# Attention feeding a gated feed-forward: the first batch's keys are finished chunk by chunk, and the first images of the main loop are reordered

## The chip, the cores and the metric

The kernel runs on one core of one Trainium2 chip. The metric is the device time of one execution in microseconds, start-up and end included; the span that a profile shows, from the first to the last instruction, is about 2 us shorter. Runs of both kernels that are compared were made on the same chip, in alternation; the experiments were spread over four chips (runs 1 to 4, 5 to 8, 9 to 11, and 12).

## The reference, cut to what matters

```python
def attention(q, kv, w_sr):                    # q: 4 x 12288 x 128, kv: 4 x 384 x 32 x 128
    kv_pool = kv.reshape(B, 96, 4, 8, 4, C).mean(axis=(2, 4))   # 4 x 4 pixels become one
    k = v = kv_pool.reshape(B, -1, C) @ w_sr                    # 768 keys a batch
    a = softmax(q @ k.T / sqrt(C))
    return a @ v

x = attention(...).reshape(49152, 128)
out = (maximum(x @ w_gate, 0) * (x @ w_val)) @ w_out            # d_ff = 1536
```

The kernel cuts the 49152 query rows into 96 tiles of 512, which it calls images. Each needs scores against six chunks of 128 keys, a product with the values, and the feed-forward part: 12 value products, 12 gate products and 48 out products. It works as a pipeline: in the main loop, the scores of image k, the values of image k-1, the value and gate products of image k-3 and the out products of image k-4 are woven together.

## The kernel before

In what follows PE is TensorE, PEld its weight loads, DVE VectorE, ACT ScalarE, POOL GpSimd. Matmul results stand in banks of PSUM, all other tiles in SBUF. A chunk is 128 keys. Before the loop there is a lead, in which the keys of the first batch come in while nothing else can be done. They come in three pairs of chunks; each pair has four lines (`dh` 0 to 3, 512 KB each), and a key is the sum over four lines and four pixels. TensorE transposes ("turns") lines into a PSUM bank in accumulating mode, which adds them up on the way; the turned sum is copied to SBUF, multiplied with `w_sr` and scaled into `kv16`.

```python
    def turn_open(b, pair):
        kv_Ts[b, pair] = bank([128, 2, 128])               # one bank for both chunks of a pair

    def turn_add(b, pair, lines, first=False, final=False, chunks=(0, 1)):
        n = lines.shape[2]
        for h in chunks:
            for i in range(n):                             # four pixels
                nc.tensor.matmul(kv_Ts[b, pair][:, h], lines[:, h, i], ident, is_transpose=True, ...)
        if final and h == 1:                               # one copy for both chunks
            kvT = work.tile([128, 2, 128], FP32, tag="kvT", bufs=2)
            nc.vector.tensor_copy(kvT, kv_Ts[b, pair])
            kv_Ts[b, pair] = kvT

    def project(b, pair):                                  # one product, one scaling for both
        pr = bank([128, 2, 128])
        nc.tensor.matmul(pr, w_sr_f32, kv_Ts.pop((b, pair)), start=True, stop=True)
        nc.vector.tensor_scalar(kv16[:, b, 2 * pair : 2 * pair + 2, 0:C], pr, 1.0 / (r * r), None, op0=ALU.mult)
# [cut]
    # pair 1: lines 0 and 1 are added on VectorE and turned; so are lines 2 and 3, half by half
    turn_open(0, 1)
    turn_add(0, 1, add_lines(1, 0, nc.vector), first=True)
    attend(0, 0)
    for h in range(2):
        s2 = add_lines(1, 2, nc.vector, slice(h, h + 1))
        turn_add(0, 1, s2, final=True, chunks=[h])
    attend(1, 0)
# [cut: loads of the feed-forward weights, queries of group 1 loaded and transposed by DMA, group 2 loaded]
    project(0, 1)
    scores_of(0, 1)
    turn_values(0, 1)
    scores_of(1, 1)
# [cut: pair 2 in the same way, further scores and values]
    for jc in range(NJC - 2):
        values(2, jc, 0)
    left = [(2, jc, 0) for jc in range(NJC - 2, NJC)]      # value steps left over for the first loop image
    left += [(k, jc, half) for k, half in ((3, 0), (2, 1), (3, 1)) for jc in range(NJC)]
# [cut]
    for k in range(LAG, last + 1):                         # the main loop; LAG is 3, the first image
        for step in range(NFB):                            # 12 steps
            kO, kF = k - LAG - 1, k - LAG
            if k == LAG and step >= NFB - 4:
                out_proj(kF, step - NFB + 4)               # 4 of the out products of image 0, early
            if k == LAG + 1 and step % 3 > 0:
                out_proj(kO, 4 + step - 1 - step // 3)     # the other 8
            if 0 <= kO:
                if kO > 0:
                    out_proj(kO, step)
            # [cut]
            if kF < NT:
                value_proj(kF, step)
            if k == LAG:
                own, left = left[:2], left[2:]
                for kV, jc, half in own:
                    values(kV, jc, half)
                    if jc == NJC - 1:
                        keep_sums(kV, half)                # reciprocal, VectorE
                        keep_values(kV, half, nc.scalar)   # normalising multiplies, ScalarE
```

The softmax here doesn't subtract the row's maximum and nothing guards it: scores larger than these inputs give would overflow.

## Time and profile before

| | before |
|---|---|
| time, median of 3 runs (of 6 with those made beside the changed kernel) | 1047.13 us (1046.61) |
| span of the profiled execution | 1044.4 us |
| TensorE busy | 1032.6 us, 99% |
| from the third loop image on | 10.52 us an image, TensorE full |

The granted clock is the share of its full clock at which TensorE ran. A page of the profile gives the busy time of each engine and the chain of work that ended last. The views by stretch, the timelines of one engine and the waits say what happened when. In a timeline, a line holds start, length, engine, source line, operation, output and input tiles with their shapes, the number of instructions in a row, and in brackets how long the engine had stood still and what released it. The reading in one sentence: the loop is TensorE-bound to a few tenths of a per cent, so only the lead and the first two loop images (some 50 us) can give anything. There, no engine is full from the last line of pair 1 to the first value product, and in the second loop image ScalarE is full while TensorE has gaps.

### The profile page before, as it was taken

The page shows a single profiled execution, that of the slowest core. Times are in us where ns is not written, and L with a number is a line of the kernel's source. Part 1 is how long each engine was busy: PE and PEld are TensorE (multiplying, and loading weights), DVE is VectorE, ACT ScalarE, POOL GpSimd, SP SyncE. Part 2 cuts the span into 40 slices and gives each one's busy share as a digit, 9 for nine tenths or more (in the row PEclk, how much of TensorE's full clock was granted, in tenths as well). Part 3 has the DMA queues.
Part 4 walks back from the last instruction along what each step waited for, and adds up shares of the span by engine and source line. Part 5 has one row for each costly group of instructions (what it writes and reads, how often), then busy time and mean ns, then how long its engine had stood idle before and what let it go on. Part 6 is the DMA issues. An engine that isn't in the chain of part 4 may idle for free.

```text
span 1044.4 us, 26093 instructions
## 1 busy us (share of the span) xinstructions
PE 1032.6 (99%) x9948; PEld 686.1 (66%) x9948; DVE 911.3 (87%) x1670; ACT 907.9 (87%) x1741; POOL 107.9 (10%) x127
## 2 busy tenths in 40 slices
PE   7999999999999999999999999999999999999998
PEld 5566666666666666666666666666666666666665
DVE  3798889898888888898888888999888888888898
ACT  3888888888888888888888888888888888888886
POOL 2000044200000005500000003440000000000000
PEclk9999999999999999999999999999999999999999
DMA  8733254432322335543224144562432322212111
GB/s 301 121 82 72 78 181 136 96 73 56 81 57 61 78 115 144 150 84 80 56 63 86 32 87 132 147 151 52 92 63 55 72 67 52 67 32 67 32 47 47
DMA packets 140254, 92.54 MB, mean 89 GB/s; under 512 B 117728, under 2 KB 118624, under 8 KB 140128
## 3 DMA queue, kind: packets, MB, share of 16 engines
q1 hardware_dynamic: 134544, 77.56, 27.7%
q0 software_dynamic: 5440, 13.24, 7.8%
q8 instruction: 78, 1.28, 0.5%
q14 instruction: 48, 0.39, 0.1%
q10 hardware_dynamic: 144, 0.07, 0.0%
HBM read 52.76 MB, written 25.17 MB: 75 GB/s over the span
## 4 chain that ended last, share of the span: by engine, by line
PE 96%; DMA 2%; SPq 1%; DVE 0%; issue 0%; ACT 0%; DVEq 0%
PE bank_ps L274 24%; PE bank_ps L264 23%; PE bank_ps L253 23%; PE bank_ps L215 12%; PE bank_ps L204 11%; DMA parts<-in_kv_dram 2%; SPq L128 1%; SPq L190 1%; PE bank_ps L168 0%; PE bank_ps L156 0%; DMA xT<-x 0%; DMA kvT<-blocks 0%; ACT aT L205 0%; SPq L93 0%; DVE kvT L163 0%
## 5 line engine op out<-in xcount | busy, mean ns | idle before, releaser
L267 DVE SCALAR_TENSOR_TENSOR hT<-bank_ps,val 128x512 f16<-128x512 f32 x1152 | 759.6, 686 | 100.8 <-ACT val L257 75.9
L257 ACT CAST val<-bank_ps 128x512 f16<-128x512 f32 x1152 | 677.9, 591 | 111.5 <-PE bank_ps L253 109.6
L274 PEld LDWEIGHTS <-hT 128*128 128x128 f16 x4608 | 353.1, 98 | 203.7 <-issue 0.9
L274 PE MATMUL bank_ps<-wo,hT 128*128 128x128 f16 x4608 | 443.6, 219 | 0.0
L253 PE MATMUL bank_ps<-xT,wv 128*128 128x512 f16 x1152 | 436.6, 379 | 0.2 <-DMA xT<-x 0.2
L264 PE MATMUL bank_ps<-xT,wg 128*128 128x512 f16 x1152 | 436.6, 379 | 0.0
L205 ACT ACTIVATE aT<-bank_ps 128x512 f16<-128x512 f32 x576 | 346.0, 604 | 17.0 <-PE bank_ps L204 16.6
L215 PE MATMUL bank_ps<-kv,aT 128*128 128x129 f16 x2304 | 223.2, 220 | 0.0
L215 PEld LDWEIGHTS <-aT 128*128 128x128 f16 x2304 | 177.2, 98 | 68.1 <-issue 0.6
L204 PE MATMUL bank_ps<-qT,kv 128*128 128x512 f16 x576 | 216.4, 379 | 1.1 <-DVE kv L169 0.5
L264 PEld LDWEIGHTS <-wg 128*128 128x128 f16 x1152 | 112.7, 98 | 65.7 <-issue 0.5
L253 PEld LDWEIGHTS <-wv 128*128 128x128 f16 x1152 | 112.7, 98 | 0.8 <-DMA xT<-x 0.3
L231 DVE TENSOR_TENSOR x<-bank_ps,rinv 128x256 f16<-128x256 f32 x188 | 79.7, 424 | 6.5
L78 POOL DMA_DIRECT2D q<-in_q_dram x23 | 12.5, 543 | 567.1 <-DMA qT<-q 567.0
L292 DVE TENSOR_SCALAR o_sb<-bank_ps 128x512 f32<-128x512 f32 (+1 forms) x95 | 64.0, 674 | 1.3 <-PE bank_ps L274 1.3
L139 POOL TENSOR_TENSOR s<-parts 128x512 f32<-128x512 f32 x36 | 45.3, 1269 | 165.1 <-DMA parts<-in_kv_dram 156.0
L204 PEld LDWEIGHTS <-kv 128*128 128x128 f16 x576 | 55.8, 98 | 2.4 <-DVE kv L169 1.4
L223 DVE RECIPROCAL rinv<-bank_ps 128x2 f32<-128x2 f32 x192 | 30.6, 160 | 1.6 <-PE bank_ps L215 1.6
L141 POOL TENSOR_TENSOR s<-s 128x512 f32<-128x512 f32 x18 | 22.8, 1267 | 1.4
L143 POOL TENSOR_TENSOR c<-s 128x256 f32<-128x256 f32 x18 | 13.1, 725 | 1.4
L168 PE MATMUL bank_ps<-kvT,w_sr_f 128*128 128x256 f32 x24 | 7.5, 393 | 2.1 <-DMA kvT<-blocks 1.2
L146 POOL TENSOR_TENSOR kv_s<-c 128x128 f32<-128x128 f32 x18 | 8.2, 455 | 1.4
(38 smaller groups left out, 64.0 us busy)
## 6 DMA issues: line engine op xcount, KB each, us to landing
parts<-in_kv_dram SPq DMA_DIRECT2D x48, 512.0 KB, 6.2
out_dram<-o_sb SPq DMA_DIRECT2D x95, 256.0 KB, 2.1
q<-in_q_dram POOLq DMA_DIRECT2D x23, 512.0 KB, 5.3
kvT<-blocks SPq DMA_DIRECT2D x144, 8.0 KB, 1.8
xT<-x SPq DMA_TRANSPOSE x94, 2.5
q<-in_q_dram SPq DMA_DIRECT2D x1, 768.0 KB, 8.3
wv<-in_moe_w_val_dram POOLq DMA_DIRECT2D x2, 192.0 KB, 4.2
wg<-in_moe_w_gate_dram POOLq DMA_DIRECT2D x2, 192.0 KB, 4.7
```

What stands on the lines that cost most here:

```text
L139: eng.tensor_tensor(s2[:, i], parts[:, 2 * i, h], parts[:, 2 * i + 1, h], op=ALU.add)
L204: nc.tensor.matmul(s_ps, kv16[:, k // NST, jc, 0:C], qT_of(k), start=True, stop=True)
L205: nc.scalar.activation(aTs[k][:, jc, :], s_ps, AF.Exp, scale=qk_scale)
L215: nc.tensor.matmul(x_ps[:, i, :], aTs[k][:, jc, s * 128 : (s + 1) * 128], kv16[:, k // NST, jc, C : 2 * C + 1], start=(jc == 0 and i == 0) ...
L223: nc.vector.reciprocal(rinvs[k, half], x_banks[k, half][:, :, C : C + 1])
L231: nc.vector.tensor_tensor(x16s[k][:, 2 * half : 2 * half + 2, :], x_ps[:, :, 0:C], rinv.to_broadcast([128, 2, C]), op=ALU.mult,)
L253: nc.tensor.matmul(va_ps, wv16[:, fb * 128 : (fb + 1) * 128], xTs[k], start=True, stop=True)
L257: nc.scalar.copy(val, va_ps)
L264: nc.tensor.matmul(g_ps, wg16[:, fb * 128 : (fb + 1) * 128], xTs[k], start=True, stop=True)
L267: nc.vector.scalar_tensor_tensor(hTs[k][:, fb, :], g_ps, 0.0, vals.pop((k, fb)), op0=ALU.max, op1=ALU.mult)
L274: nc.tensor.matmul(o_ps, hTs[k][:, fb, s * 128 : (s + 1) * 128], wo16[:, fb, :], start=first, stop=(fb == NFB - 1), skip_group_check=True,)
L292: nc.vector.tensor_scalar(o_sb, o_ps, 1.0 / X_SCALE**2, None, op0=ALU.mult)
```

## The change

The intent is to shorten the way from a landed line to the first score on its keys, and to spread the loop's first two images so that neither ScalarE nor TensorE has idle bits. It has six parts:

1. Every chunk has a bank, a copy, a product and a scaling of its own.
2. In pairs 1 and 2 the last two lines are turned directly from their landed form. VectorE's sums (lines 0 and 1, and then half of the pixels) no longer touch a late line. GpSimd's share of the sums in pair 2 goes to VectorE.
3. The last scores of the lead stand among the first value products.
4. A normalising multiply of the first loop image is issued a step after its reciprocal.
5. The out products of image 0 all stand in the second loop image.
6. The warm-up uses eight matmuls of 512 columns for 34 of 128, and four such matmuls, called fillers below, stand in waits of the first lines.

```diff
-    def turn_open(b, pair):
-        kv_Ts[b, pair] = bank([128, 2, 128])
...
+    def turn_end(chunk, lines):
+        turn_add(chunk, lines)
+        if chunk % 2 == 0:
+            kv_Ts["pair"] = work.tile([128, 2, 128], FP32, tag="kvT", bufs=2, name="kvT")
+        kvT = kv_Ts["pair"][:, chunk % 2]
+        nc.vector.tensor_copy(kvT, kv_Ts[chunk])
+        kv_Ts[chunk] = kvT
+
+    def project_chunk(jc):
+        pr = bank([128, 128])
+        nc.tensor.matmul(pr, w_sr_f32, kv_Ts.pop(jc), start=True, stop=True)
+        nc.vector.tensor_scalar(kv16[:, 0, jc, 0:C], pr, 1.0 / (r * r), None, op0=ALU.mult)
...
+    def first_lines(pair, dh=0):
+        s2 = work.tile([128, 2, r, C], FP32, tag="kv_s2", bufs=3, name="kv_s2")
+        nc.vector.tensor_tensor(s2, line(pair, dh), line(pair, dh + 1), op=ALU.add)
+        s1 = work.tile([128, r, C], FP32, tag="kv_s1", bufs=2, name="kv_s1")
+        s1 = s1.rearrange("p (h i) c -> p h i c", h=2)
+        nc.vector.tensor_tensor(s1, s2[:, :, 0:2], s2[:, :, 2:4], op=ALU.add)
+        return s1
...
+    s1 = first_lines(1)
+    for h in range(2):
+        turn_add(2 + h, line(1, 2, h), first=True)
+    for h in range(2):
+        turn_add(2 + h, s1[:, h])
+    for h in range(2):
+        turn_end(2 + h, line(1, 3, h))
+    for h in range(2):
+        for half in range(2):
+            values(0, h, half)
+        project_chunk(2 + h)
+    scores_of(0, 1)
+    turn_values(0, 1)
+    scores_of(1, 1)
+    gate = const.tile([128, 1], FP32)
+    nc.gpsimd.tensor_copy(gate, line(2, 2)[:, 0, 0, 0:1])     # holds the weights' loads back
...
+    late = [(2, 5), (3, 4), (3, 5)]
+    left = {0: [(1, jc, half) for jc in range(NJC - 2, NJC) for half in range(2)]}
+    for step, k, half in ((1, 2, 0), (4, 3, 0), (7, 2, 1), (10, 3, 1)):
+        left[step] = [(k, jc, half) for jc in range(NJC // 2)]
+        left[step + 1] = [(k, jc, half) for jc in range(NJC // 2, NJC)]
...
-            if k == LAG and step >= NFB - 4:
-                out_proj(kF, step - NFB + 4)
-            if k == LAG + 1 and step % 3 > 0:
-                out_proj(kO, 4 + step - 1 - step // 3)
             if 0 <= kO:
-                if kO > 0:
-                    out_proj(kO, step)
+                out_proj(kO, step)
...
+            if k * NFB + step in ready:
+                kV, hV = ready.pop(k * NFB + step)
+                keep_values(kV, hV, nc.scalar)
             if k == LAG:
+                if late:
+                    scores(*late.pop(0))
...
+                        if kV == 1:
+                            keep_values(kV, hV)
+                        else:
+                            ready[k * NFB + step + 1] = (kV, hV)
```

## The prediction

> **What bounds the kernel now.** I read the page first: shares of the engines, then the chain that ended last.
>
> ```profile
> PE 1032.6 (99%) x9948; PEld 686.1 (66%) x9948; DVE 911.3 (87%) x1670; ACT 907.9 (87%) x1741; POOL 107.9 (10%) x127
> ...
> PE 96%; DMA 2%; SPq 1%; DVE 0%; issue 0%; ACT 0%; DVEq 0%
> ```
>
> TensorE is busy for 99% of the span and carries 96% of the chain. A change that removes none of its matmuls can only win time in which it waits. So I cut the first 61 us into stretches, at points that exist in both kernels: first kv line landed (5.29), last line of pair 1 landed (17.42), first score of pair 2 (27.18), first value product (31.94), start of the second and third image of the main loop (40.89, 50.25).
>
> ```profile
> 0.00:5.29 5.29, 3.33 (x34) 3.16 (x35) 0.06 (x1) 1.49 (x2) 1.35 (x8) 1.00 0.59 188
> 5.29:17.42 12.13, 9.49 (x71) 6.44 (x72) 5.12 (x12) 3.72 (x8) 0.00 (x0) 1.00 1.00 394
> 17.42:27.18 9.76, 8.32 (x67) 5.80 (x64) 4.67 (x9) 4.55 (x9) 6.09 (x8) 1.00 0.87 230
> 27.18:31.94 4.76, 4.39 (x47) 2.86 (x47) 2.01 (x8) 4.08 (x8) 0.00 (x0) 1.00 1.16 184
> 31.94:40.89 8.95, 8.91 (x87) 5.82 (x85) 7.27 (x18) 7.09 (x18) 0.53 (x1) 1.00 1.01 159
> 40.89:50.25 9.36, 9.17 (x67) 4.96 (x66) 8.00 (x13) 9.36 (x21) 0.00 (x0) 1.00 0.43 74
> 50.25:60.77 10.52, 10.52 (x101) 6.85 (x100) 9.51 (x17) 9.77 (x20) 0.53 (x1) 1.00 0.57 109
> ```
>
> The columns are stretch, length, then busy time of PE, PEld, DVE, ACT, POOL, and granted clock, DMA share, GB/s. To 17.42 the DMA runs at its full 394 to 430 GB/s; nothing can be quicker than its lines. From 17.42 to 31.94 no engine is full: this is latency. From 40.89 to 50.25 ACT is full (9.36 of 9.36). From 50.25 on an image costs 10.52 us, all of it PE. So the end is 994 us after the mark at 50.25, and the question is how far that mark, the first value product of the third image, moves. I call it R. The TensorE work ahead of R is the same set in both kernels, but for four line turns more.
>
> Next, in the order of time, the waits between 17 and 28 us:
>
> ```profile
> 17.51 1.29 DVE L362 TENSOR_TENSOR kv_s<-parts 128x512 f32<-128x512 f32 x2 [1.30 <-DMA parts<-in_kv_dram]
> 19.55 0.42 DVE L163 COPY kvT<-bank_ps 128x256 f32<-128x256 f32 x1 [0.75 <-PE bank_ps L156]
> 20.83 0.42 DVE L169 TENSOR_SCALAR kv<-bank_ps 128x256 f16<-128x256 f32 x1
> 21.74 3.24 ACT L205 ACTIVATE aT<-bank_ps 128x512 f16<-128x512 f32 x6 [4.00 <-PE bank_ps L204]
> 23.61 0.69 DVE L362 TENSOR_TENSOR kv_s<-parts 128x512 f32<-128x512 f32 x1 [1.25 <-DMA parts<-in_kv_dram]
> 27.61 4.50 ACT L205 ACTIVATE aT<-bank_ps 128x512 f16<-128x512 f32 x8 [0.89 <-PE bank_ps L204]
> ```
>
> From landing to first score of pair 1: 17.42 to 21.31, or 3.9 us, through an add of each half (0.69), eight turns, a copy of 256 columns, the product and a scaling of 256; ACT stood still for 4.00. For pair 2: 23.49 to 27.18, 3.7 us. Last, the first image of the loop on ACT:
>
> ```profile
> 35.72 0.63 ACT L229 ACTIVATE x<-bank_ps,rinv 128x128 f16<-128x128 f32 x2 [0.58 <-DVE rinv L223]
> ...
> 38.25 0.63 ACT L229 ACTIVATE x<-bank_ps,rinv 128x128 f16<-128x128 f32 x2 [0.46 <-DVE rinv L223]
> ...
> 40.78 0.63 ACT L229 ACTIVATE x<-bank_ps,rinv 128x128 f16<-128x128 f32 x2 [0.46 <-DVE rinv L223]
> ```
>
> A normalising multiply stands in ACT's queue ahead of the casts and waits for a reciprocal that DVE takes after its products: three steps take 2.53 us (35.72 to 38.25), where ACT alone needs 1.95.
>
> **What the Trainium skill says.** "TensorE: Matmul & The Clock Gate", Part 1, gives starts 106.7 or 426.7 ns apart at 128 or 512 columns on the cold clock, 55.6 or 215.7 once warm, after some 3.4 us of work. The trace agrees: 107 ns between the first 25 warm-up matmuls, then 56; scores 216 apart. The f32 turns start 109 apart, measured here. "PSUM — Partial Sum Buffer", section "PSUM bank collisions raise a hardware error", says that two engines may not touch one bank and quadrant at once. That is why before, with both chunks in one bank, the copy waits for the second chunk, and why own banks are needed to overlap; the trace fits (copy at 19.55, after the eighth turn). "ScalarE: Activation LUTs", section "What ACT_TABLE_LOAD costs", puts an immediate-scale ACTIVATE at 186 ns + 0.833 ns a column, less about 93 back to back: 520 for 512 columns by that; the trace has 0.48 to 0.50, which I use.
>
> **The change, part by part.** Durations from the rows above and their neighbours; a DVE op of 128 columns I estimate at 0.29 us, starts 0.20 apart, from 0.42 at 256 and 0.69 at 512.
>
> Warm-up: eight matmuls of 512 columns end at 1.72 + 6 x 0.427 + 2 x 0.216 = 4.7, as before; the four fillers (0.43 us a pair) lie in waits for lines at 9.14 and the cast at 8.13. Worth nothing.
>
> Pair 0, line landed 10.40: chunk 0's turns end 11.11, copy to 11.43, product to 11.95, scaling to 12.27; the score of chunk 0 at 12.33 in place of 13.28. But the next scores wait for the other queries, landed at 12.31, whose three casts now come behind the scalings; the eight exps end near 17.6 against 17.74. So this part gives almost nothing.
>
> Pair 1: the pixel sums (1.22 + 0.6) run 15.4 to 17.2, ahead of line 3 (17.42). Line 2 is turned at 16.2 to 17.1, the sums 17.3 to 17.75, line 3 to 18.6; copies 18.4 and 18.8, products 18.85 and 19.35, scalings 19.3 and 19.85. First score at 19.7 against 21.31, second 20.2: about 1.4 us won, because one add of a late line left the chain and the halves overlap.
>
> Pair 2: line (2,2) landed 22.24 and (2,3) 23.49, against steps of 1.28 until then: 1 us late. The trace has one 16 KB packet of the instruction queue at 19.92, 1.09 us long, and one data engine finishing that much after the rest. It came after 256 TensorE records; the new lead reaches 256 only near the turning of the last line, so I expect landings near 21.3 and 22.5. Then DVE sets it: the sums start after the copy of the values, 21.0, end 22.8; four turns to 23.3, two scores, line 3 turned 23.7 to 24.6, copies 24.4 and 24.8, products, scalings 25.3 and 25.8, scores at 25.7 and 26.1 against 27.18. With late landings 0.5 later: 1.0 to 1.5 us won.
>
> Then exps to 27.1, the values of image 0 to 27.8, two reciprocals and two products (1.0), turning and copy to 29.8: first value product at 29.8 against 31.94, since image 1's last part no longer stands before it. What was left out there is not saved: it goes into the loop.
>
> First loop image, TensorE: 24 products x 0.216 + 28 value steps x 0.113 + 3 scores x 0.216 + 4 turns = 9.2 us (before 8.5 by the same sum, 8.95 measured). ACT: 12 casts x 0.47 + 3 exps x 0.48 + 8 multiplies x 0.265 = 9.2. DVE: 12 x 0.60 + 1.6 = 8.8. The three are level; the multiply, moved one step on, no longer holds ACT for 0.5 us each.
>
> Second loop image: TensorE 24 x 0.216 + 6 x 0.216 + 48 x 0.056 = 9.1; ACT 18 x 0.48 = 8.6. Before, out products had gone to the first image and ACT was the bound with 9.36 for the same stretch. Spread as now, TensorE is.
>
> Sum: R = 29.8 + 9.2 + 9.1 = 48.1; I add 0.6 for stalls where three engines are within 5% of each other: 48.7. Against 50.25 that is 1.55 us, and some 0.3 us of small stalls after R (gaps to 52 us, ACT behind) should go too. **About 1.8 us of 1047.13: 1045.3 us, 0.17%.**
>
> **Rivals.** ACT stays the bound: from the first exp of pair 2 (26.1) it has 9 exps, 24 casts, 6 exps, 8 multiplies left, 22 us by the durations above, so it cannot be done before 48.1, and each idle bit after 26.1 (I count some 1.0, around the wait for the first value product) pushes R. Then R near 49.3: 1046.2. For it: 9.36 of 9.36 above; against: R comes about a microsecond before ACT's own end.
>
> A DMA takes the place of the latency: the transposed queries of the second group landed at 39.13, first needed at 41.46. The new lead needs them at about 39.7, and the weights' start hangs on a POOL copy that waits for line (2,2). If that lands late (22.24), the queries land near 39.7: the gain shrinks by 0.3 to 0.8, 1045.9. Against: with line (2,2) at 21.3 the weights start 0.35 earlier than at 21.84.
>
> The gain is given back: what PE won is lost to the extra line turns (4 x 0.109), separate products and dense ends of the loop image; 1047.0. Against: the 4.00 us ACT wait is real and shrinks. The opposite, the new lead with no stall and the landings early: 1044.5.
>
> **Range and chances.** The median of before comes from runs 1.0 us apart, so 0.5 us of noise either way; stalls and landings give 0.7. Range 1044.2 to 1046.5. Two per cent are 21 us; the whole lead before the mark loses about 14 us of TensorE time (50.25 less 36 of work), 5.3 of them before the first line. So faster by over 2% is all but out; slower by as much would need a stall at every image, which nothing in the loop after R gives cause for.
>
> **What would show it.** Right: first score of pair 1 near 19.7, of pair 2 near 25.7, first value product near 29.8, R near 48.7; ACT's three-step period in the first loop image near 2.0 and not 2.53; an image still 10.52 after R. Wrong: landings of the last lines not moved, a score of the fifth image waiting for the queries' transpose, ACT idle for a reciprocal as before, a cold clock inside the lead, or the mark moved and the end not.

## The result, and the profile after

The changed kernel took 1045.23 us, the median of six runs (1043.80 to 1045.81); the kernel before 1046.61, the median of six (1046.12 to 1047.39). The medians differ by 1.38 us. The ratio is 0.9984, with a 95% interval from 0.9971 to 0.9997: within 2%, and just outside no change. A ratio here is the mean time of one kernel's fast runs over the mean of the other's in the same rounds, so it isn't quite the ratio of the medians.

The page of the changed kernel has the same picture as before. With the four extra line turns, the separate products and the fillers, TensorE's busy time is 1.1 us longer:

```profile
PE 1033.7 (99%) x9936; PEld 686.2 (66%) x9936; DVE 912.5 (87%) x1676; ACT 908.0 (87%) x1741; POOL 107.2 (10%) x127
```

The lead, cut at the same marks as in the prediction (last line of pair 1 landed 18.88, first score of pair 2 27.27, first value product 31.23, second loop image 40.68, third 49.83), with the same columns: stretch, length, busy time of PE, PEld, DVE, ACT and POOL, then granted clock, DMA share and GB/s:

```profile
5.08:18.88 13.80, 11.62 (x76) 7.93 (x76) 6.13 (x15) 3.98 (x8) 0.00 (x0) 1.00 1.01 386
18.88:27.27 8.39, 7.78 (x65) 6.09 (x66) 4.16 (x10) 3.90 (x8) 4.55 (x7) 1.00 0.62 179
27.27:31.23 3.96, 3.34 (x38) 2.34 (x37) 1.97 (x7) 3.27 (x6) 0.73 (x2) 1.00 1.11 195
31.23:40.68 9.45, 9.45 (x92) 6.25 (x91) 7.99 (x19) 8.89 (x21) 0.00 (x0) 1.00 1.23 177
40.68:49.83 9.15, 9.15 (x81) 5.57 (x79) 7.77 (x14) 9.09 (x21) 0.54 (x1) 1.00 0.54 89
49.83:60.35 10.52, 10.52 (x106) 6.98 (x103) 9.42 (x17) 9.74 (x20) 0.53 (x1) 1.00 0.63 116
```

Three things are to be seen. In the two first loop images TensorE is now full (9.45 of 9.45, 9.15 of 9.15), while ScalarE is busy for 8.89 and 9.09. Before, TensorE had 8.91 of 8.95 and 9.17 of 9.36, and ScalarE was full in the second (9.36 of 9.36). The stretch from the last line of pair 1 to the first score of pair 2 is 8.39 us for 9.76. And the first stretch is longer, 13.80 for 12.13: the key lines landed later in this execution.

Those landings differ from one execution to the next. So I measure all marks from L, the landing of the last line of pair 0 (10.40 us before, 11.84 in the changed kernel), and add what the prediction gives when its own L, 10.40, is taken off:

| us after L | before | predicted | changed | difference |
|---|---|---|---|---|
| first score of pair 1 | 10.91 | 9.3 | 9.34 | -1.57 |
| first score of pair 2 | 16.78 | 15.3 | 15.43 | -1.35 |
| first value product | 21.54 | 19.4 | 19.39 | -2.15 |
| third loop image begins (R) | 39.85 | 38.3 | 37.99 | -1.86 |
| from R to the end of the span | 994.15 | 993.85 | 993.57 | -0.58 |

The spans of the two profiled executions differ by 1.0 us: L came 1.44 later, R - L is 1.86 shorter, and the rest 0.58 shorter. In that rest, one wait, TensorE for the block transposes of the second batch's keys at some 186 us, took 1.21 us before and 0.64 after, which is as much as the whole difference (more on this rest at the end).

Where the time between the line and the scores went, VectorE from the pixel sum of pair 1 to the sums of pair 2:

```profile
18.01 0.69 DVE L375 TENSOR_TENSOR kv_s<-kv_s 128x512 f32<-128x512 f32 x1
19.89 0.73 DVE L163 COPY kvT<-bank_ps 128x128 f32<-128x128 f32 x2 [1.18 <-PE bank_ps L153]
20.83 0.29 DVE L169 TENSOR_SCALAR kv<-bank_ps 128x128 f16<-128x128 f32 x1 [0.21 <-PE bank_ps L168]
...
22.21 0.29 DVE L182 COPY kv<-bank_ps 128x256 f16<-128x256 f16 x1 [0.59 <-PE bank_ps L181]
22.42 1.22 DVE L372 TENSOR_TENSOR kv_s<-parts 128x1024 f32<-128x1024 f32 x1
23.68 0.69 DVE L375 TENSOR_TENSOR kv_s<-kv_s 128x512 f32<-128x512 f32 x1
```

No add stands between the line of pair 1 (18.88) and the copies (19.89); from line to first score it is 2.30 us, for 3.89 before. The sums of pair 2 follow right behind the copy of pair 1's values (22.21): VectorE's queue, not the landing of the last lines, sets when pair 2 can be turned. The answering lines of ScalarE:

```profile
21.60 2.08 ACT L210 ACTIVATE aT<-bank_ps 128x512 f16<-128x512 f32 x4 [2.58 <-PE bank_ps L209]
...
27.70 1.10 ACT L210 ACTIVATE aT<-bank_ps 128x512 f16<-128x512 f32 x2 [1.28 <-PE bank_ps L209]
...
35.43 0.63 ACT L234 ACTIVATE x<-bank_ps,rinv 128x128 f16<-128x128 f32 x2
...
37.46 0.63 ACT L234 ACTIVATE x<-bank_ps,rinv 128x128 f16<-128x128 f32 x2
```

The wait for pair 1 fell from 4.00 to 2.58. The normalising multiplies have no bracket any more, they wait for nothing, and are 2.03 us apart for 2.53.

### The profile page after: what moved, and what is told of

Same layout as the page of the kernel before. It is cut to its first block, busy times and chain, and to the rows that moved or that the text cites. A ratio compares the mean times of both kernels' runs of the same rounds, so it can differ in the third digit from the quotient of the medians.

```text
span 1043.4 us, 26070 instructions
## 1 busy us (share of the span) xinstructions
PE 1033.7 (99%) x9936; PEld 686.2 (66%) x9936; DVE 912.5 (87%) x1676; ACT 908.0 (87%) x1741; POOL 107.2 (10%) x127
## 4 chain that ended last, share of the span: by engine, by line
PE 95%; DMA 2%; SPq 1%; DVE 0%; issue 0%
PE bank_ps L279 24%; PE bank_ps L258 23%; PE bank_ps L269 23%; PE bank_ps L220 12%; PE bank_ps L209 11%; DMA parts<-in_kv_dram 2%; SPq L128 1%; SPq L195 1%; DMA xT<-x 0%; PE bank_ps L153 0%; PE bank_ps L173 0%; DMA kvT<-blocks 0%; DVE kv_s L372 0%; SPq L93 0%; PE bank_ps L168 0%
## 5 line engine op out<-in xcount | busy, mean ns | idle before, releaser
L153 PEld LDWEIGHTS bank_ps<-ident,parts 128*128 128x128 f32 x64 | 7.9, 154 | 3.2 <-DMA parts<-in_kv_dram 2.3
L153 PE MATMUL bank_ps<-ident,parts 128*128 128x128 f32 x64 | 9.3, 296 | 0.7 <-DMA parts<-in_kv_dram 0.4
```

## The experiments

The predicted time was met, but so could a sum of errors be. The theory is that of the prediction: the gain is made between line and score in pairs 1 and 2 and between first value product and R, and each part of the change gives its share. The rivals: the gain is only where lines happened to land; a transfer (the transposed queries of the second group) takes the place of the latency; or the warm-up and the fillers have an effect that the prediction denied. Twelve runs were made. Each was timed against the kernel before in rounds of its own; all gave correct results.

### 1. The changed kernel once more

No edit. It shows how far the marks repeat.

> The changed kernel once more, unaltered. In its first profile the loads from the first query part on landed some 1.4 us late (line 3 of pair 0 at 11.84 against 10.40 in the kernel before), and it still reached the mark R (first value product of the third image) 0.42 us sooner. Theory A, the prediction's: that lateness is a data engine falling behind by chance, and the marks hang on the landings. Then a run whose last kv line lands near 22.6 has its first score of pair 2 near 25.8, first value product near 29.9, R near 48.6; in any run R less the landing of the last line is near 26 us (before: 26.8). Rival B: the new order itself makes the loads late, so the last line lands at 23.9 again. Rival C: ACT sets R, so that R stays near 49.8 wherever the lines land. Time 1 to 2 us under before.

Measured: 1044.89 us (5 runs) against 1046.66 for before (9), ratio 0.9990 [0.9977, 1.0002]. First value product at L + 19.40, so the same within 0.01. But R came at L + 39.30, 1.31 later, and the cause is one wait on TensorE at the first score of the fifth image:

```profile
40.86 0.38 PE L258 MATMUL bank_ps<-xT,wv 128*128 128x512 f16 x1
...
42.37 0.39 PE L209 MATMUL bank_ps<-qT,kv 128*128 128x512 f16 x1 [1.13 <-DMA qT<-q]
```

The second rival is real. The transposed queries landed at 42.32, 1.46 us after the stage began. With that wait (1.29 against the execution without it) taken off, R is at L + 38.01. Of the nine profiles of the new lead that don't change this load, six show the wait, from 0.27 to 1.40 us; over the nine it is 0.60 in the mean. The execution of the changed kernel in the section above happened to have none: there the queries landed at 40.83 and were needed at 40.90.

### 2. The new lead with the old loop part

The edit, condensed:

```diff
-    late = [(2, 5), (3, 4), (3, 5)]
-    left = {0: [(1, jc, half) ...
+    scores_of(2, 2); x_turn_pe(0); scores_of(3, 2); attend(1, 2)
+    for half in range(2):
+        keep_sums(1, half); keep_values(1, half)
+    ... # values, normalising and out products as in the kernel before
```

> The new lead up to the first score of pair 2, but from there the order of before: all scores and image 1's last values ahead of the first value product, normalising multiplies at once, four output steps of the first image in the first loop image. Theory A: the first value product comes as long after the first score of pair 2 as before (4.8 us, against 4.0 in the changed kernel), ACT again takes 2.5 us for three steps of the first loop image, and the second image is bound by ACT at 9.3; the mark R is 0.8 to 1.3 us later, measured from the last landing, than in the changed kernel. Rival C (ACT's total work sets R, the order does not matter): R less the last landing is the same within 0.3 us.

Measured: 1045.30 us, ratio 0.9991 [0.9977, 1.0004]. By stretch, from the first value product:

```profile
32.44:41.39 8.95, 8.91 (x88) 5.83 (x85) 7.28 (x18) 7.09 (x18) 0.53 (x1) 1.00 1.14 177
41.39:50.74 9.35, 9.16 (x67) 4.95 (x66) 7.99 (x13) 9.35 (x21) 0.00 (x0) 1.00 0.45 74
```

These are the kernel before's two images almost to the hundredth (8.95 and 9.36), ScalarE full in the second. First value product at L + 20.85 (1.46 later than with the change), the two images together 18.30 (0.30 less): the loop part is worth 1.16 us at R. It moves work behind the first value product, and the loop takes it in for a fifth of what it saves ahead.

### 3. VectorE adds the last two lines again

The edit, condensed. It also leaves out the pixel sums of lines 0 and 1, which the kernel before hadn't either, so it undoes part 2 as a whole:

```diff
+    def last_lines(pair, h, ...):      # line 2 plus line 3 of one half, VectorE
+        nc.vector.tensor_tensor(s2[pair][:, h], line(pair, 2, h), line(pair, 3, h), op=ALU.add)
-        turn_add(2 + h, line(1, 2, h), first=True)
-        turn_add(2 + h, s1[:, h])
-        turn_end(2 + h, line(1, 3, h))
+        turn_add(2 + h, s1[:, h], first=True)
+        turn_end(2 + h, last_lines(1, h))          # and so for pair 2
```

> The changed kernel with the last two lines of pairs 1 and 2 summed on DVE before they are turned, as before, instead of turned directly; own banks, products and copies kept. Theory A: one add of a late line (0.69 us, and the second chunk's 0.60 behind it) comes back between the last landing and the first score: from the landing of the last line of pair 2 to its first score 3.6 to 4.2 us in place of 3.35, and for pair 1 2.9 to 3.4 in place of 2.3. Rival: in pair 2 the pixel sums, not the late line, are the last to be ready, so direct turning wins nothing there (3.35 again).

Measured: 1044.71 us, ratio 0.9993 [0.9976, 1.0009]. First score of pair 1 at L + 10.02 (0.68 later, one add of 0.69), of pair 2 at L + 15.88 (0.45), first value product 19.85 (0.46), R 38.84, or 38.46 less its query wait of 0.38. Direct turning is worth 0.47 at R. The part of the theory that said "one add leaves the chain" holds with its size.

### 4. Both chunks of a pair in one bank

The edit, condensed:

```diff
-            kv_Ts[chunk] = bank([128, 128])
+            kv_Ts["both"] = bank([128, 2, 128])     # one copy, one product, one scaling for two
```

> The changed kernel with one bank, one copy of 256 columns, one product and one scaling for the two chunks of a pair, as before; everything else kept. Theory A: the first score of a pair comes later by about 0.5 us (the copy waits for the second chunk's four turns, 0.44; copy, product and scaling are each some 0.13 to 0.2 longer), the second score comes with it and so 0.1 us later to 0.2 sooner than now. Rival: since both chunks' scores are needed before the values of image 0, only the second counts, and the own banks win nothing at the first value product (within 0.15 us, measured from the last landing).

Measured: 1045.82 us, ratio 0.9996 [0.9983, 1.0010]. First score of pair 1 at L + 10.74, 1.40 later; R at L + 39.86, 1.87 later, with no wait for queries. That is far more than the half microsecond I had given to this part. VectorE shows how it comes:

```profile
17.14 0.69 DVE L378 TENSOR_TENSOR kv_s<-kv_s 128x512 f32<-128x512 f32 x1
19.46 0.42 DVE L162 COPY kvT<-bank_ps 128x256 f32<-128x256 f32 x1 [1.62 <-PE bank_ps L153]
20.73 0.42 DVE L170 TENSOR_SCALAR kv<-bank_ps 128x256 f16<-128x256 f32 x1 [0.85 <-PE bank_ps L169]
```

The copy begins at L + 8.98 (8.05 with own banks): 0.93. About half of that is not the copy's own wait. The pixel sum of pair 1 begins at L + 6.66 for 6.17, 0.49 later, since pair 0 in one bank has already held up VectorE's queue, and the turns follow it; the other 0.44 are the second chunk's four turns, for which the copy now waits. From copy to scaling it is 1.27 for 0.94, since the product stands behind the values of both chunks rather than of one: 0.33. The scaling takes 0.42 for 0.29: 0.13. These three make 1.39 of the 1.40. And the delay isn't absorbed at pair 2 (first score 2.03 later after L), because pair 2's sums stand in VectorE's queue behind pair 1's values. So own banks pay mostly through what they allow in TensorE's order, not through the copy itself.

### 5. The sums of pair 2 one place earlier in VectorE's queue

If VectorE's queue, and not the lines, sets pair 2, the sums can go ahead of the copy of pair 1's values.

```diff
     scores_of(0, 1)
+    s1 = first_lines(2)
     turn_values(0, 1)
     scores_of(1, 1)
...
-    s1 = first_lines(2)
```

> A version meant to beat both: the pixel sums of pair 2's first two lines are issued on DVE ahead of the copy of pair 1's turned values, which made DVE wait 0.59 us for PE. In the changed kernel's profile the sums were ready at 24.37 and the last line had landed at 23.92. Theory A (sums and landing set pair 2): sums ready 0.8 us sooner, the first score of pair 2 follows the last landing by 2.6 to 2.9 us in place of 3.35 and the first value product, R and the end come about 0.5 us sooner measured from the landing. Rival C (ACT sets R): the first score moves, R does not (within 0.15 us).

Measured: 1044.43 us, ratio 0.9981 [0.9968, 0.9995]. First score of pair 2 at L + 14.83 (0.60 sooner), first value product L + 18.79 (0.60 sooner). That confirms the queue. But R came at L + 38.80, 0.81 later than in the changed kernel, by stretch:

```profile
30.26:39.71 9.45, 9.45 (x92) 6.26 (x91) 7.99 (x19) 8.89 (x21) 0.00 (x0) 1.00 1.29 185
39.71:50.27 10.56, 9.32 (x81) 5.57 (x79) 8.20 (x14) 9.86 (x21) 0.54 (x1) 1.00 0.46 80
```

The second image took 10.56, TensorE busy for 9.32 of it: the query wait again, 1.40. What is won ahead of a fixed landing is paid back at the landing.

### 6. The normalising multiply not put off

The edit, condensed:

```diff
-                            ready[k * NFB + step + 1] = (kV, hV)
+                            keep_values(kV, hV, nc.scalar)
```

> The changed kernel with the normalising multiply of images 2 and 3 issued at once instead of one step on. Theory A: ACT waits about 0.5 us for the reciprocal at each of the four multiplies, three steps take 2.5 us in place of 2.0, the first loop image is 1.0 to 2.0 us longer than 9.45. Rival: the other buffers take it up and the image stays within 0.4 us.

Measured: 1045.43 us, ratio 0.9994 [0.9980, 1.0007]. The old period of 2.53 us is back on ScalarE, with the wait for the reciprocal:

```profile
35.92 0.63 ACT L234 ACTIVATE x<-bank_ps,rinv 128x128 f16<-128x128 f32 x2 [0.46 <-DVE rinv L228]
...
38.45 0.63 ACT L234 ACTIVATE x<-bank_ps,rinv 128x128 f16<-128x128 f32 x2 [0.46 <-DVE rinv L228]
```

The two images take 9.69 and 9.91 (9.45 and 9.15 with the change). So the 1.0 to 2.0 us that I had expected in the first of them did not come: it is 0.24, within the rival's 0.4. R is at L + 39.00: 1.01 later, of which 0.27 is the query wait, so 0.74 by the deferral itself. ScalarE's idle bits cost little in the image where they lie (0.24) and more in the next one (0.76, with the query wait in it). That the casts put off there are the cause is my reading, not shown.

### 7. The out products of image 0 as before

```diff
+            if k == LAG and step >= NFB - 4:
+                out_proj(kF, step - NFB + 4)
+            if k == LAG + 1 and step % 3 > 0:
+                out_proj(kO, 4 + step - 1 - step // 3)
             if 0 <= kO:
-                out_proj(kO, step)
+                if kO > 0:
+                    out_proj(kO, step)
```

> The changed kernel with the output steps of the first image spread as before (four in the first loop image, eight in the second). Theory A: the first loop image takes 0.87 us more (four steps of 0.218), the second is bound by ACT at 8.6 to 8.8 instead of 9.15, so R is 0.3 to 0.6 us later. Rival: the sum is the same work and R stays within 0.15 us.

Measured: 1044.72 us, ratio 0.9984 [0.9969, 0.9999]. The images take 10.12 and 9.32, R is at L + 38.83, and 0.80 of that is the query wait. Less the wait it is 38.03, 0.04 from the changed kernel, and the next image takes 10.67 for 10.52. But a wait of 0.8 right there hides whatever the shift does before it, so what this part is worth at R isn't settled. The 0.15 in the next image repeats: that image takes 10.67 in all five profiles with the old placing of the out products (before, runs 2, 7, 11 and 12), and 10.52 in eight of the nine with the new one (10.63 in run 6).

### 8. The old warm-up, without fillers

The edit, condensed:

```diff
-    fill(8)                 # matmuls of 512 columns, and two pairs of fillers among the first lines
+    fill(34)                # of 128 columns, and none
```

> The changed kernel with the warm-up of before (34 matmuls of 128 columns) and without the four fillers. Prediction: the fillers are worth nothing: the f32 turns stay 109 ns apart, no score is later, measured from the landings, by more than 0.15 us. And 20 more TensorE instructions stand ahead, so the first 16 KB packet of the instruction queue comes earlier than 21.5 us, near 19.5 to 20.5; if it is what made the lines late in the kernel before, the last two lines land about 1 us late again (steps of over 2 us once, in place of 1.28). Rival: the lateness is chance, and all steps stay near 1.28 with the packet at the earlier place.

Measured: 1045.60 us, ratio 0.9994 [0.9980, 1.0007]. First value product at L + 19.41, R at L + 39.27, or 38.02 less a query wait of 1.25. In the profiled execution the fillers were worth nothing, as predicted. It also brought back a late line: one packet of 16 KB on the DMA queue that the profile calls instruction began at 20.34, and line (2,2) landed 1.88 us after line (2,1), for 1.24 to 1.28 in the twelve profiles where that packet began at 21.34 or later. Before has the same at 19.92, with a step of 2.25. So "the packet makes a line late" holds for these two. That it costs anything doesn't: from the first score of pair 1 to that of pair 2 it is 5.87 us in the kernel before with the late line and 5.86 in run 11 below without it, and 6.09 to 6.11 in the changed kernel and in runs 1, 6 and 8, whichever way the lines landed.

### 9. The third group's queries loaded after the second group's transpose

Why does the transpose land late? Its load is issued at the same place in the order of lines as before, but in the new lead the weights' loads, and with them everything on that queue, start 0.35 us later after L. GpSimd's copy of one column, which holds them back, shows why. The changed kernel and run 5, timelines of GpSimd:

```profile
22.72 0.96 POOL L421 COPY gate<-parts 128x1 f32<-128x1 f32 x1 [20.70 <-DMA parts<-in_kv_dram]
```

```profile
22.36 0.19 POOL L422 COPY gate<-parts 128x1 f32<-128x1 f32 x1 [20.34 <-DMA parts<-in_kv_dram]
```

The same copy took 0.96 us beside VectorE's add of 1024 columns (22.42 to 23.64, in the timeline above) and 0.19 in run 5, where that add had run from 21.16 to 22.38. The Trainium skill, "SBUF — State Buffer", section "Who interferes with whom", names just this pair: a VectorE operation with two SBUF inputs and a GpSimd operation that reads SBUF, of which the later one waits. The trace agrees for the GpSimd copy: in all seven profiles in which it began inside that add (it then took 0.33 to 0.97 us) it ended 0.04 to 0.06 us after the add, and in the other four it took 0.18 to 0.19. The reverse can't be seen: in runs 5 and 10 VectorE's next add, of 512 columns, began beside the copy and took 0.69 and 0.70 us, as elsewhere.

But this start doesn't decide when the queries land. In runs 3, 4 and 5, whose copy took 0.19, the second group's load was issued at L + 13.26 to 13.29, for 14.03 or 14.04 in the other six profiles of the nine; the transposed queries landed at L + 29.7 to 29.8 all the same, for 28.6 to 30.5 in the six. What varies is the transpose itself: it takes 6.7 to 8.5 us from issue to landing while the third group's queries are loaded beside it. So I held that load back until the transpose had landed:

```diff
+    gate2 = const.tile([128, 1], FP32)
+    nc.gpsimd.tensor_copy(gate2, qTs[1][:, 0, 0:1])
     q_load(2)
```

> The changed kernel, in which the load of the queries of group 2 waits on POOL until the transposed queries of group 1 have landed (a copy of one column), instead of running beside that transpose. Five of nine profiles of the new order show the first score of the fifth image waiting for that transpose (landed 40.8 to 42.3, 14.9 to 16.5 us after the load's issue, against a need at about the first value product + 9.65); the transpose of group 2, with nothing beside it, took 4.4 us from issue to landing, that of group 1 7.1 to 8.5. Theory D (the new bound is this transpose, slowed by the load beside it): landing comes within 12 to 13 us of the load's issue, no wait, second loop image 9.15 us, R less the last landing 25.9 us or less (27.2 in the repeat). Rival: the transpose is slow by itself or by the other traffic, lands after 14.5 us or more, and R is not better than in the repeat.

Measured: 1044.24 us against 1045.66 for before in the same rounds, ratio 0.9987 [0.9974, 0.9999]. The queries landed at 39.38, 13.56 us after the load's issue (14.95 to 16.55 in the changed kernel, runs 1 and 5; 12 to 13 had been expected), the transpose's part 5.4. After L that is 27.59, sooner than in any of the nine profiles. No wait, R at L + 38.00. By this one trace the wait is gone (three of the nine had none either); by time alone this run can't be told from the changed kernel, whose ratio is 0.9984.

### 10. Both: sums earlier and the load held back

```diff
     scores_of(0, 1)
+    s1 = first_lines(2)
     turn_values(0, 1)
...
+    gate2 = const.tile([128, 1], FP32)
+    nc.gpsimd.tensor_copy(gate2, qTs[1][:, 0, 0:1])
     q_load(2)

-    s1 = first_lines(2)
```

> Early pixel sums for pair 2 and the later load of group 2's queries together. If theories A and D hold, the sums' gain now reaches the end: first value product 6.7 us after the last landing as with the sums alone, second loop image 9.15 instead of 10.56, R near 25.3 us after the last landing, and the time about 1 us under the changed kernel: 1043.0 to 1044.0, against before 0.997. If ACT sets R (rival C), R stays 25.9 us after the landing.

Measured: 1043.13 us (5 runs, 1042.68 to 1043.36), ratio 0.9973 [0.9961, 0.9986]: the quickest of all the kernels, and its slowest run is ahead of every run of before in the same rounds (lowest 1045.28). By stretch:

```profile
30.27:39.72 9.45, 9.45 (x92) 6.26 (x92) 8.00 (x19) 8.89 (x21) 1.20 (x3) 1.00 1.04 135
39.72:48.87 9.15, 9.15 (x81) 5.60 (x79) 7.76 (x14) 9.09 (x21) 0.00 (x0) 1.00 0.72 139
```

The queries landed at 37.56 (L + 26.10), no wait, and R is at L + 37.41, 0.58 ahead of the changed kernel. The 0.60 that run 5 won and lost again now arrives. It also refutes the rival in which ScalarE sets R, in the form put down before runs 5 and 10: R did not stay where it was. The form in the prediction, about 22 us of ScalarE's work after the first exp of pair 2, isn't refuted: that exp came sooner as well, and from it to R it is 22.14 us here (26.73 to 48.87) and 22.13 in the changed kernel (27.70 to 49.83). In the second image TensorE (9.15 of 9.15) and ScalarE (9.09) are both all but full; which of them sets its length was not tested.

### 11. The kernel before with the short warm-up

```diff
-    idle = bank([128, 128])
-    for _ in range(34):
-        nc.tensor.matmul(idle, ident16, ident16, start=True, stop=True)
+    filler = const.tile([128, 512], FP16)
+    nc.vector.memset(filler, 1.0)
+    idle = bank([128, 512])
+    for _ in range(8):
+        nc.tensor.matmul(idle, ident16, filler, start=True, stop=True)
```

It has 52 fewer TensorE instructions ahead of the lines (26 matmuls and their weight loads), which was to move the instruction packet and so the late line, with the rest of the old lead as it was.

> The kernel before with eight warm-up matmuls of 512 columns in place of 34 of 128: 52 TensorE instructions fewer ahead of the lines, nothing else. If the 16 KB instruction packet made its last two lines late (step of 2.25 us at 19.92), the packet now comes later, near 21.5 to 22.5, all steps are 1.24 to 1.30, and the last line lands 10.6 us after line 2 of pair... in fact 12.1 us after line 3 of pair 0 (13.09 before); the first score of pair 2 follows 0.5 to 1.0 us sooner, so part of the change's gain is the shorter warm-up alone. Rival: a late step again with no packet near it. Also: if line 2 of pair 0 lands after 9.6 here too, that first lateness (10.56 in the changed kernel, 9.14 in before) is chance and not the new order.

Measured: 1047.44 us (4 runs), ratio 1.0017 [1.0002, 1.0032]. The packet moved to 21.86 and the late line was gone (all steps within pairs 1 and 2 from 1.24 to 1.29; the last line landed 12.08 after L, for 13.09). And R - L is 39.84, for 39.85: the last lines coming a microsecond sooner after L changed nothing. In this pair of profiles the first rival fails: with landings as early as the changed kernel's, the old lead has none of the gain. Why this kernel is 0.17% slower is open; two of its four runs had a mean clock of 0.997 to 0.998, which the next run bears on.

### 12. The kernel before once more

No edit.

> The kernel before, unaltered, timed against itself (ratio 1.000 within the interval) and profiled again. Two things are open. The landing of line 3 of pair 0 was 10.40 and 10.92 us in the two profiles of the old lead, 10.48 to 12.01 (mean 11.4) in eleven of the new: if it comes at 11 or later here, the old lead draws from the same lot; at 10.4 to 10.7 rival B (the new order makes the first loads later) stays possible. And the mark R less that landing should be 39.85 us again, as in the two old-lead profiles so far (39.85 and 39.84), whatever the landing.

Measured: 1047.79 us (4 runs) against 1046.29 (7) for the same kernel as the reference of the rounds, ratio 1.0005 [0.9982, 1.0029]: the same, as it must be. But the profiled execution (1047.77) had R at L + 41.19, 1.34 later than before, and this is why, by stretch:

```profile
7.50:11.20 3.70, 1.49 (x12) 1.08 (x12) 0.85 (x2) 0.00 (x0) 0.00 (x0) 1.00 1.02 418
11.20:15.00 3.80, 3.21 (x13) 2.45 (x14) 0.80 (x3) 0.00 (x0) 0.00 (x0) 0.52 1.02 417
15.00:19.00 4.00, 3.91 (x22) 2.03 (x19) 3.52 (x8) 2.08 (x5) 0.00 (x0) 0.60 1.03 410
```

The granted clock (third number from the end) fell to half at 11.375 us, for 6.83 us, after a stretch in which TensorE had been busy for 1.49 of 3.70 us. The longest gap in that stretch was 1.64 us. How little is too little isn't shown: in run 8, also without fillers, TensorE was busy for 1.61 us of 3.70 (7.48 to 11.18) and the clock held. So I went through the mean clock of every execution for which it was listed. Kernels with fillers (the changed one, runs 1 to 7, 9 and 10): 46 executions, none under 0.999. Kernels without (before in all its rounds, runs 8, 11 and 12): 46 executions, 10 of them at 0.996 to 0.998. The kernel before took 1048.05 us in the mean of its seven such executions, and 1045.98 in the other 31. Only one of these drops was seen in a trace; that the rest fell in the lead too is likely from the same size, but not shown.

That the fillers prevent the drop is not shown either, for the chips differ. Six of the ten low executions are of the 11 on the chip of run 12, where no kernel with fillers ran. On the chips of runs 1 to 11 it is 4 in 35 without fillers (1 of 27 of the kernel before, 1 of 4 in run 8, 2 of 4 in run 11) and 0 in 40 with them (the chip of the changed kernel's first six isn't listed).

## Why the prediction was right

**The time and the marks.** 1045.3 was predicted and 1045.23 measured. But the prediction took 1.8 us off 1047.13, and in the rounds with the changed kernel the kernel before stood at 1046.61: the gain is 1.38 us by the medians, 1.68 by the means. Half a microsecond of the agreement is thus the reference's own shift. The steps hold: with the landing L taken off, the four marks of the lead are met within 0.31 us, three of them within 0.15 (the table above). In absolute times they are 1.1 to 1.6 us off (first score of pair 1 at 21.18 for 19.7, R at 49.83 for 48.7), because the prediction took the landings of one execution as given. Over eleven profiles of the new lead, L runs from 10.48 to 12.01 (mean 11.37), over three of the old one from 10.40 to 11.22. Whether the new order delays the line or it is chance can't be told from three.

**Pair 1.** 1.6 us at the first score was predicted, 1.57 measured. The reasons hold (run 3: one add, 0.68 at the first score; run 4: own banks, 1.40). They don't add up to it, and at R the parts undone one by one (0.47, 1.87, 1.16 for the loop part) come to more than the 1.86 in all: each relies on the others' order, and an undone part leaves an order that the kernel before never had. That own banks are needed for the overlap, as the prediction takes from the page on PSUM, no run tests: the old copy waits for both chunks because it is one instruction over both.

**Pair 2.** The first branch of the sum, "Then DVE sets it", was right (run 5), and 1.5 of that branch became 1.35. The second branch, "With late landings 0.5 later", was wrong. In run 8 line (2,2) landed at L + 11.46, 0.63 later than in the changed kernel, and the first score of pair 2 stood at L + 15.44 for 15.43; in the old lead (run 11) landings a microsecond earlier changed nothing either. The premise that the packet comes after 256 TensorE records failed too: it came after 252 records in the kernel before and 256 in run 8, but after 207 to 227 in the other new leads and 237 in run 12. That it makes a line late was right for the two that began before 21 us.

**The loop images.** 9.2 + 9.1 + 0.6 for stalls gave 18.9; 9.45 + 9.15 = 18.60 was measured, TensorE full in both, with ScalarE's period at 2.03 for the predicted 2.0. The allowance for stalls was 0.3 too large. "ACT stays the bound" gave R near 49.3, which is 38.9 after the L that it assumed, and 37.99 was measured. But its ingredients hold: ScalarE's last cast of these images ended 0.68 us after R, with 0.88 us of idle time since the first exp of pair 2. In the second image the two engines can't be told apart (run 10).

**After R.** Some 0.3 us was predicted to go. In the two profiles 0.58 went: 0.15 in the first image after R (10.67 to 10.52), 0.57 in the wait for the second batch's block transposes, which the prediction hadn't seen, and 0.19 after the last value product, while other images gave 0.3 back. That wait was over 0.5 us in two of three profiles of the old lead and in one of eleven of the new. From R to the end it is 993.9 us in the mean of the three and 992.6 in the mean of the eleven. So more may go after R than the prediction or these two profiles say; it was seen and not tested, and three are few.

**The queries.** The rival "A DMA takes the place of the latency" came true in part, and against my reason: the weights start at L + 11.79 and not 0.35 us earlier than before's L + 11.44, but 0.35 later. The step that failed is that the copy which releases them was taken at 0.19 us (21.3 to 21.49); it costs 0.96 beside VectorE's add. A second step failed with it: an earlier start does not by itself bring the queries sooner (runs 3 to 5), because the transpose is slow beside the next load. The wait takes 0.60 us in the mean of nine profiles (runs 1 and 5; none in runs 9 and 10, where the load is held back), within the 0.3 to 0.8 that the rival named.

**The fillers.** "Worth nothing" is true while the clock holds (run 8). Whether they keep it up is open: on the chips where both kinds ran, 4 of 35 executions without them and none of 40 with them had a lower clock. If that is their doing they are worth about 0.15 us a run, by my estimate (4 / 35 x 1.34, the loss in run 12), and nearer 0.05 against the kernel before itself (1 of 27). The warm-up's sum was off, harmlessly: all eight matmuls ran 0.427 us apart, and the turns began at 5.12, not 4.7, just after their line (5.08).

**So the agreement to 0.1 us is luck in part.** R came 0.3 sooner after L than predicted in the first profile, and more went after R; the queries take 0.6 away in the mean, the kernel before had moved by 0.5, and L differs by up to 1.5 us between executions. The sum closes within the 0.5 us that the prediction allowed for noise, and no closer.

## What to carry to other kernels

When a kernel is bound by one engine for 99% of its span, measure a change of its lead at the mark where the steady loop begins, relative to the landing that starts the chain; the time alone, with runs 1 to 3 us apart, doesn't show parts of half a microsecond. Here own banks for the halves of a piece of work paid by letting the other engines' queues interleave with them, and a delay in one such chain passed to the next through the queue of the engine that they share (0.49 us from pair 0 to pair 1 in run 4). After each gain ask which transfer is needed next: 0.6 us won ahead of it arrived only when the transfer came sooner too. And before counts from several machines are pooled, split them by machine: of ten low-clock executions six were on one chip.

## What the Trainium skill lacked or had wrong

- "TensorE: Matmul & The Clock Gate", Part 1, ties the fall to the half clock to an idle window of about 3.4 us and, in the section on oscillation, gives a rule of no idle gaps over that. Here the clock halved for 6.83 us with no gap over 1.64 us, after TensorE had been busy 1.49 of 3.70 us (run 12), and held in run 8 after 1.61 of 3.70. The page speaks of short idles elsewhere, but a busy share at which the clock falls isn't stated.
- "DMA: Bandwidth & Descriptors" doesn't say what instruction refills cost the transfers beside them, nor does another page. Here one packet of 16 KB took 1.0 to 1.2 us; when it began at 19.92 or 20.34, a 512 KB line landed 0.6 to 1.0 us late (steps of 1.88 and 2.25 for 1.28), and when it began at 21.34 or later, beside the last lines too, none did. Why is open.
- The same page on DMA has bandwidths for DMA transposes, but not what a load beside one does to it: 6.7 to 8.5 us from issue to landing with one (twelve profiles), 5.4 and 4.7 without (runs 9 and 10).
